# Sixteen output buffers in the weight staging tiles, and nine stores issued late

## Chip, core and metric

The kernel runs on one core of a Trainium2 chip. The metric is the device time of one execution in microseconds (us). TensorE (PE in the profile; its weight loads are PEld) multiplies matrices and writes PSUM, VectorE (DVE), ScalarE (ACT) and GpSimd (POOL) work on elements, and SyncE (SP) issues all DMAs, one after the other, each once the data that it moves is ready and the place that it writes is free.

## What is computed

A gated linear attention over 4 batches, 8 heads, 768 steps and a head width of 48, whose output is the input of a layer with a squared ReLU:

```python
for t in range(S):
    state = alpha[:, :, t, :, None] * state + np.einsum('bhd,bhe->bhde', k[:, :, t], v[:, :, t])
    y[:, :, t] = np.einsum('bhd,bhde->bhe', q[:, :, t], state)
...
x = np.ascontiguousarray(attn_out.transpose(0, 2, 1, 3)).reshape(B * S, H * D)
h = x @ w_in                # 3072 x 384 times 384 x 2048
r = np.maximum(h, 0.0)
g = s * (r * r) + b
return g @ w_out            # 3072 x 2048 times 2048 x 384
```

Inputs and output are float32; the kernel multiplies in bf16.

## The kernel before

The 3072 tokens are cut into 24 blocks of 128, six to a batch. The recurrence is done in blocks: cumulated products of alpha (`cumA`) scale q and k (`eb1`, `ei1`, then the multiplies `mul1` on line 609, which write the bf16 tile `qk`), the scores of a block are k times q under a triangular mask (`A1`, line 652, then `mk1`), and a state of 48 x 48 per head goes from block to block (`KV1`, `t1`, `sn`). The first eight blocks are handled in pairs by functions that end in 2 (`ld2`, `mul2`, `A2`, `mk2`, `y2`); from block 8 on each stands by itself. For the scores, q and k are needed with the head width on the partitions. For blocks 0 to 5 TensorE transposes them (`T2`); for blocks 6 and up a DMA transpose does, issued by SP (`T1`, line 630, from `qk` to `qkT`). `y1` forms the block's output in two PSUM banks and `ye` copies it to `xd`.

Blocks go through the layer two at a time (`GROUPS`). `mm1` multiplies by `w_in` into two PSUM banks `h_ps`, `re` (line 756) takes the ReLU into one of three tiles `r`, `sq` (line 775) squares it into `gt`. `mm2` (line 780) multiplies a block by `w_out` in four calls of four matmuls into `o_ps[n % 2]`. `oe(n)` (line 789, VectorE) scales that bank, adds the bias and writes it to an output buffer in SBUF, and `st(n)` stores the buffer: as two DMAs of 96 KB for blocks 0 to 7 (line 829), whose rows are interleaved, as one of 192 KB for the others (line 834). The last block is done in two halves of 192 columns (`mm2h`, `oeh`, `sth`). There are three output buffers `o_sb`, and block n uses the one with number n % 3, so `oe(n)` waits until `st(n - 3)` has landed.

The weights come in float32 through staging tiles: four tiles `wst` of 128 x 1536, of which the first two serve twice, and parts of two `gt` tiles. ScalarE, GpSimd and VectorE cast them to bf16 (`cih`, `co`) and sum `w_out` for the bias (`cp`). After about 44 us nothing touches `wst` any more.

The order of all this is written out by hand: the string `PROGRAM` lists every step, and a loop at the end of the kernel calls the function that each entry names (`mul1.q.12.DVE` is `mul1("q", 12, "DVE")`). Each engine runs its own instructions in that order and waits at each one for what it needs; the waits are derived from the regions of tiles that instructions read and write. Entries of different engines can change places in the string with no effect on either engine's order.

`F.n.w.bank` issues n matmuls of w columns on zeros into a bank that is rewritten afterwards: fillers, which keep TensorE at work while the first loads arrive.

Of the kernel before, what the change touches and what calls it, by code (L numbers as in the profile page):

```python
# [70 lines left out]
KV1.10 sq.3.3.0.ACT mm2.5.3 mul1.q.11.DVE re.3.2.1.1.ACT mm2.4.2 ld1.k.12 oe.5 sq.3.2.1.POOL mm2.4.3
ld1.v.11 t1.10 T1.11 A1.9 ln2.7 sn.10.POOL oe.4 mm2.7.0 mk1.9 mm2.7.1 ld2.a.11 mm2.6.0 ld1.k.13 st.3
mm2.6.1 Ayy.10 ld2.a.8 mm2.7.2 ld1.v.13 ye.8.DVE ye.9.ACT vc1.12.POOL mk1.10 mm1.4.1.0 vc1.11.POOL
mm1.4.2.1 re.4.1.0.2.ACT blk2.6 cumA.6 re.4.2.1.0.ACT A1.11 sq.4.2.0.DVE ei1.12 mm1.4.4.0 eb1.12
mul1.k.12.DVE mm1.4.3.1 eb1.13 mul1.q.12.DVE re.4.4.0.1.ACT mm2.6.2 mul1.q.13.DVE T1.12 el2.6
re.4.3.1.0.ACT sq.4.1.2.DVE mm1.4.0.0 sq.4.4.1.DVE sq.4.3.0.DVE mm1.4.6.1 re.4.0.0.2.ACT st.4 mk1.11
mm2.6.3 ei1.13 ld1.q.15 re.4.6.1.1.ACT mm1.4.7.0 sq.4.0.2.DVE ld1.v.14 oe.6 KV1.12 vc1.13.POOL mm2.7.3
t1.12 mm1.4.5.1 mul1.k.13.DVE mm2.8.0 T1.13 re.4.5.1.0.ACT Ayy.12 re.4.7.0.2.ACT oe.7 ld1.q.16 mm2.8.1
ld1.k.14 ye.10.DVE ye.11.ACT st.5 sq.4.5.0.DVE blk2.7 KV1.13 mk1.12 mm1.5.4.1 ld1.k.15 mm2.9.0 ld1.v.15
vc1.14.POOL re.5.4.1.0.ACT t1.13 mm1.5.5.0 sq.4.7.2.DVE mm1.5.6.1 sq.5.4.0.DVE re.5.5.0.2.ACT  # L80
sq.4.6.1.DVE cumA.7 sn.13.POOL ld1.v.16 A1.13 el2.7 mm1.5.3.0 re.5.6.1.0.ACT mk1.13 eb1.14 ld2.a.9
mm2.9.1 ei1.14 mul1.q.14.DVE ei1.15 mm2.8.2 re.5.3.0.1.ACT sq.5.6.0.DVE mm1.5.1.1 mul1.k.14.DVE eb1.15
sq.5.3.1.DVE mm2.8.3 T1.14 re.5.1.1.0.ACT mm1.5.0.0 sq.5.1.0.DVE sq.5.5.2.DVE mm1.5.2.1 st.7
re.5.0.0.1.ACT mul1.q.15.DVE mm2.9.2 oe.8 ld1.k.17 re.5.2.1.0.ACT sq.5.0.1.DVE st.6 KV1.14 mm1.5.7.0
mul1.k.15.DVE sq.5.2.0.DVE mm2.10.0 T1.15 re.5.7.0.2.ACT t1.14 mm2.10.1 sq.5.7.2.DVE sn.14.POOL mm2.10.2
ld1.k.16 ld2.a.10 Ayy.14 vc1.15.POOL ld1.v.22 ld1.q.17 mm2.10.3 ye.12.ACT mk1.14 vc1.16.POOL st.8
ye.13.ACT mm2.9.3 ln2.8 oe.10 KV1.15 mm1.6.4.1 t1.15 mm1.6.1.0 re.6.4.1.1.ACT sn.15.POOL blk2.8 cumA.8
re.6.1.0.0.ACT ld1.q.22 sq.6.4.1.DVE A1.15 eb1.16 mm1.6.3.1 oe.9 ei1.16 sq.6.1.0.DVE mm1.6.0.0
mul1.k.16.DVE re.6.3.1.2.ACT mul1.q.16.DVE mm2.11.0 el2.8 eb1.17 sq.6.3.2.DVE T1.16 re.6.0.0.1.ACT
mm2.11.1 mk1.15 ei1.17 mm1.6.2.1 sq.6.0.1.DVE ld1.v.17 mm2.11.2 re.6.2.1.0.ACT ld1.k.18 KV1.16 mm2.11.3  # L90
ld1.q.18 t1.16 st.10 mm1.6.6.0 oe.11 mm1.6.5.1 re.6.6.0.2.ACT mm2.13.0 ln2.10 sq.6.6.2.DVE mul1.q.17.DVE
mm1.6.7.0 re.6.5.1.1.ACT mul1.k.17.DVE Ayy.16 re.6.7.0.2.ACT T1.17 sq.6.7.2.DVE sq.6.2.0.DVE mm2.12.0
ye.14.ACT ye.15.DVE vc1.17.POOL ld1.v.18 ln2.9 mk1.16 sn.16.POOL mm2.13.1 ld1.q.23 ld1.q.19 mm1.7.0.1
sq.6.5.1.DVE ld1.k.19 blk2.9 mm1.7.4.0 re.7.0.1.2.ACT st.9 sq.7.0.2.DVE mm1.7.6.1 re.7.4.0.0.ACT
mm2.13.2 sq.7.4.0.DVE re.7.6.1.1.ACT cumA.9 A1.17 ld1.v.19 eb1.18 mm1.7.1.0 ei1.19 mul1.q.18.DVE
mm2.12.1 el2.9 eb1.19 mk1.17 vc1.18.POOL ei1.18 mm2.12.2 re.7.1.0.2.ACT mm1.7.7.1 mul1.k.18.DVE ln2.11
sq.7.1.2.DVE T1.18 mm2.13.3 re.7.7.1.0.ACT mm1.7.2.0 oe.13 mm2.12.3 ld1.k.20 mul1.q.19.DVE
re.7.2.0.2.ACT ld1.q.20 mm1.7.3.1 sq.7.2.2.DVE ld1.q.21 mul1.k.19.DVE mm2.15.0 re.7.3.1.2.ACT oe.12
vc1.19.POOL T1.19 mm1.7.5.0 sq.7.3.2.DVE KV1.18 mm2.14.0 re.7.5.0.2.ACT t1.18 st.11 mm2.14.1 ld1.k.21
sq.7.7.0.DVE sq.7.5.2.DVE Ayy.18 sq.7.6.1.DVE ld1.v.20 mm2.15.1 ye.16.ACT ye.17.DVE ld1.v.21 mk1.18  # L100
st.12 KV1.19 mm1.8.5.1 ld1.k.22 blk2.10 mm1.8.6.0 re.8.5.1.0.ACT t1.19 mm1.8.7.1 sq.8.5.0.DVE
re.8.6.0.2.ACT sn.19.POOL cumA.10 re.8.7.1.1.ACT A1.19 sq.8.6.2.DVE mm1.8.3.0 ei1.20 sq.8.7.1.DVE
mul1.k.20.DVE mm2.14.2 re.8.3.0.0.ACT mk1.19 mm1.8.2.1 el2.10 eb1.20 mm1.8.0.0 mul1.q.20.DVE
re.8.2.1.2.ACT vc1.20.POOL mm2.15.2 T1.20 eb1.21 re.8.0.0.1.ACT sq.8.2.2.DVE mm2.14.3 sq.8.3.0.DVE
ei1.21 sq.8.0.1.DVE mm1.8.1.1 ld1.k.23 mul1.k.21.DVE st.13 oe.14 vc1.21.POOL KV1.20 mm2.15.3
re.8.1.1.2.ACT mm1.8.4.0 sq.8.1.2.DVE oe.15 mm2.16.0 re.8.4.0.0.ACT mul1.q.21.DVE st.15 mm2.17.0 t1.20
T1.21 mm2.17.1 sq.8.4.0.DVE sn.20.POOL Ayy.20 ld1.v.23 st.14 mm2.17.2 ye.19.DVE vc1.22.POOL ye.18.DVE
mm2.17.3 mk1.20 KV1.21 blk2.11 mm1.9.5.1 t1.21 mm1.9.1.0 re.9.5.1.1.ACT sn.21.POOL A1.21 re.9.1.0.2.ACT
cumA.11 mm1.9.3.1 sq.9.5.1.DVE ei1.22 eb1.22 mul1.k.22.DVE mm2.16.1 re.9.3.1.0.ACT mul1.q.22.DVE
mm2.16.2 ei1.23 oe.17 T1.22 eb1.23 mm1.9.0.0 sq.9.3.0.DVE sq.9.1.2.DVE KV1.22 mul1.q.23.DVE mm2.16.3  # L110
re.9.0.0.1.ACT mm1.9.2.1 sq.9.0.1.DVE mk1.21 mm1.9.4.0 re.9.2.1.0.ACT mm2.19.0 mul1.k.23.DVE
re.9.4.0.2.ACT oe.16 mm1.9.7.1 el2.11 T1.23 sq.9.2.0.DVE mm1.9.6.0 t1.22 re.9.7.1.1.ACT mm2.18.0 st.16
sq.9.4.2.DVE re.9.6.0.0.ACT sn.22.POOL Ayy.22 vc1.23.POOL mm2.18.1 ye.21.DVE ye.20.DVE mm2.18.2
sq.9.7.1.DVE mm1.10.4.1 mk1.22 mm2.19.1 re.10.4.1.2.ACT sq.9.6.0.DVE mm1.10.1.0 A1.23 re.10.1.0.1.ACT
# [6 lines left out]
re.11.0.1.2.ACT mm2.21.3 sq.11.0.2.DVE re.11.3.0.1.ACT sq.11.7.0.DVE mm1.11.5.1 sq.11.3.1.DVE oe.21
mm1.11.4.0 re.11.5.1.2.ACT st.21 mm2.20.3 re.11.4.0.0.ACT mm2h.23.0.0 oe.20 mm2h.23.0.1 mm2h.23.1.1
sq.11.4.0.DVE st.20 mm2.22.0 sq.11.5.2.DVE mm2h.23.1.0 mm2.22.1 mm2.22.2 mm2.22.3 mm2h.23.2.0 oe.22
mm2h.23.3.0 mm2h.23.2.1 st.22 oeh.23.0 mm2h.23.3.1 sth.23.0 oeh.23.1 sth.23.1
# [4 lines left out]
def kernel(  # L129
# [657 lines left out]

    def oe(n):
        nc.vector.scalar_tensor_tensor(  # L789
            out=out_sb[n % 3],  # L790
            in0=o_ps[n % 2][:, 0:d_model],
            scalar=s_col,
            in1=bias_w,
            op0=ALU.mult,
            op1=ALU.add,
        )
# [13 lines left out]
    def oeh(n, h):  # L810
        w = slice(d_model // 2 * h, d_model // 2 * (h + 1))
        nc.vector.scalar_tensor_tensor(
            out=out_sb[n % 3][:, w],
            in0=(o_ps[1], ct_ps)[h][:, 0 : d_model // 2],
            scalar=s_col,
            in1=bias_w[:, w],
            op0=ALU.mult,
            op1=ALU.add,
        )
# [56 lines left out]
```

## Time and profile before

| | us |
|---|---|
| median of 3 runs | 185.15 (185.14 to 186.47) |
| the profiled execution | 184.67 |
| its span, first to last instruction | 183.0 |

The profile is of one execution. Its views used here are: the page (busy time of each engine, the span in 40 slices with the rate of DMA, and the chain of work that ended last); the busy time of each engine in chosen stretches, where a row has the stretch, its length, then for each engine the busy time and the number of instructions, the granted clock of TensorE as a share of full speed, the DMA share and GB/s; and the timeline, whose rows have the start, the duration, engine, line, operation, the tile written and the tiles read, the shapes, and how many such instructions follow each other. In square brackets stands how long the engine was idle before, and what released it; buffer numbers are left out. For SP a row is the issue of a DMA, not the transfer. A wait for several things is put down to the one that came last.

### The profile page before, as it was taken

How to read it: one execution, taken by the hardware profiler on the slowest of the kernel's cores; microseconds unless marked ns; L12 is line 12 of the kernel's file. 1: busy time of each engine (PE TensorE's matmuls, PEld its weight loads, DVE VectorE, ACT ScalarE, POOL GpSimd, SP SyncE). 2: the span in 40 equal slices, each digit the busy share in tenths (PEclk: the TensorE clock that was granted, in tenths of full speed). 3: DMA queues.
4: the chain of work that ended last, by engine and by line, in shares of the span. 5: the costliest groups of instructions: out<-in, count | busy, mean ns of one | idle time of the engine just before them, and what ended most of it. 6: DMA issues, size and time to landing. Idle time of an engine off the chain costs nothing.

```text
span 183.0 us, 5543 instructions
## 1 busy us (share of the span) xinstructions
PE 171.8 (94%) x2293; PEld 122.4 (67%) x2293; DVE 133.7 (73%) x257; ACT 103.8 (57%) x202; POOL 45.5 (25%) x81
## 2 busy tenths in 40 slices
PE   7868899999999999896999999999999999999993
PEld 2436686786567775684776677777776776687772
DVE  2599989999586786593987777677986896672423
ACT  3945888998727582662383757483571552263610
POOL 7447619340332534201303202110223103000000
PEclk9999999999999999999999999999999999999999
DMA  5999999999998989999989999888957323021022
GB/s 159 323 355 378 265 345 362 364 287 238 214 198 169 178 170 213 167 239 155 227 165 231 207 203 229 159 186 162 216 134 195 81 57 104 0 86 48 0 90 86
DMA packets 101357, 34.96 MB, mean 191 GB/s; under 512 B 94548, under 2 KB 99796, under 8 KB 101332
## 3 DMA queue, kind: packets, MB, share of 16 engines
q1 hardware_dynamic: 101332, 34.61, 79.5%
q8 instruction: 18, 0.29, 0.6%
q14 instruction: 7, 0.06, 0.1%
HBM read 25.17 MB, written 4.72 MB: 163 GB/s over the span
## 4 chain that ended last, share of the span: by engine, by line
PE 71%; SPq 11%; DMA 10%; DVE 4%; ACT 2%; issue 1%; ACTq 0%
PE o_ps L780 30%; PE h_ps L746 28%; SPq L299 9%; DMA qkT<-qk 6%; DMA wst<-in_moe_w_in_dram 4%; PE a_ps L652 2%; PE py_ps L674 2%; PE ct_ps L585 1%; PE ct_ps L674 1%; DVE colsum L364 1%; DVE qk L452 1%; SPq L325 1%; PE py_ps L639 1%; DVE gt L775 1%; ACT r L756 1%; SPq L312 1%
## 5 line engine op out<-in xcount | busy, mean ns | idle before, releaser
L756 ACT ACTIVATE r<-h_ps 128x512 bf16<-128x512 f32 x88 | 52.3, 599 | 49.0 <-PE h_ps L746 40.1
L746 PE MATMUL h_ps<-xd,w_in_bf 128*128 128x256 bf16 x576 | 74.2, 273 | 0.1
L780 PE MATMUL o_ps<-w_out_bf,gt 128*128 128x384 bf16 x368 | 69.9, 326 | 0.2 <-DVE gt L775 0.2
L746 PEld LDWEIGHTS <-w_in_bf 128*128 128x128 bf16 x576 | 54.1, 98 | 13.4 <-issue 1.3
L780 PEld LDWEIGHTS <-gt 128*128 128x128 bf16 x368 | 34.5, 98 | 18.9 <-DVE gt L775 0.5
L775 DVE TENSOR_TENSOR gt<-r 128x512 bf16<-128x512 bf16 x72 | 31.2, 452 | 12.1 <-ACT r L756 11.5
L725 POOL TENSOR_TENSOR s_st<-t,blast 128x384 bf16<-128x384 bf16 x15 | 13.5, 903 | 41.3 <-DVE t L715 33.2
L661 DVE TENSOR_TENSOR am<-a_ps,U 128x1024 bf16<-128x1024 f32 x16 | 19.5, 1218 | 2.7 <-PE a_ps L652 2.7
L789 DVE SCALAR_TENSOR_TENSOR o_sb<-o_ps,bs,bias_w 128x384 f32<-128x384 f32 x23 | 14.1, 615 | 8.0 <-PE o_ps L780 4.9
L340 POOL CAST vp<-v_in 128x384 bf16<-128x384 f32 x18 | 9.3, 522 | 35.8 <-DMA v_in<-in_v_dram 26.7
L399 ACT ACTIVATE la<-a_in 128x768 bf16<-128x768 f32 x12 | 10.1, 842 | 4.5 <-DMA a_in<-in_alpha_dram 4.5
L773 ACT ACTIVATE gt<-r 128x512 bf16<-128x512 bf16 x18 | 11.1, 625 | 0.3
L715 DVE TENSOR_TENSOR t<-py_ps,s_st 64x192 bf16<-64x192 f32 x26 | 9.1, 352 | 2.9 <-PE py_ps L639 2.5
L775 POOL TENSOR_TENSOR gt<-r 128x512 bf16<-128x512 bf16 x6 | 6.2, 1039 | 19.7 <-ACT r L756 19.7
L609 DVE TENSOR_TENSOR qk<-k_in,binv 128x384 bf16<-128x384 f32 x16 | 8.8, 553 | 1.9 <-ACT binv L599 1.8
L609 DVE TENSOR_TENSOR qk<-q_in,b_s 128x384 bf16<-128x384 f32 x16 | 8.7, 550 | 1.5 <-ACT b_s L595 1.5
L514 DVE TENSOR_TENSOR am<-a_ps,mask 128x1024 bf16<-128x1024 f32 x6 | 7.3, 1217 | 2.0 <-PE a_ps L501 1.9
L652 PE MATMUL a_ps<-qkT 64*128 64x128 bf16 x128 | 6.3, 218 | 2.4 <-DMA qkT<-qk 1.9
L652 PEld LDWEIGHTS <-qkT 64*128 64x128 bf16 x128 | 3.9, 94 | 6.6 <-DMA qkT<-qk 4.2
L452 DVE TENSOR_TENSOR qk<-q_in,b_s 128x384 bf16<-128x384 f32 x8 | 4.3, 551 | 4.2 <-ACT b_s L429 4.2
L340 DVE CAST xd<-ct_ps 128x384 bf16<-128x384 f32 x6 | 3.3, 555 | 5.2 <-PE ct_ps L674 5.2
L338 ACT ACTIVATE xd<-ct_ps 128x384 bf16<-128x384 f32 x6 | 2.9, 488 | 7.0 <-PE ct_ps L674 4.7
(123 smaller groups left out, 188.2 us busy)
## 6 DMA issues: line engine op xcount, KB each, us to landing
a_in<-in_alpha_dram SPq DMA_DIRECT2D x12, 384.0 KB, 4.6
wst<-in_moe_w_in_dram SPq DMA_DIRECT2D x4, 768.0 KB, 7.6
v_in<-in_v_dram SPq DMA_DIRECT2D x16, 192.0 KB, 4.0
k_in<-in_k_dram SPq DMA_DIRECT2D x16, 192.0 KB, 3.7
q_in<-in_q_dram SPq DMA_DIRECT2D x16, 192.0 KB, 3.9
out_dram<-o_sb SPq DMA_DIRECT2D x15, 192.0 KB, 2.3
out_dram<-o_sb SPq DMA_DIRECT2D x18, 96.0 KB, 3.0
q_in<-in_q_dram SPq DMA_DIRECT2D x4, 384.0 KB, 5.9
```

The lines of the kernel that those rows point to most:

```text
L299: nc.sync.dma_start(out=to[r], in_=of[r])
L340: {"DVE": nc.vector, "POOL": nc.gpsimd}[eng].tensor_copy(out=out, in_=in_)
L609: on(eng).tensor_tensor(out=half_of(qk, n)[:, "qk".index(x), :, 0:D], in0=half_of(ins[x], n).rearrange("a (h d) -> a h d", d=D), in1=half_ ...
L652: nc.tensor.matmul(out=a_ps[:, e, 128 * p : 128 * p + 128], lhsT=T[r, 1, p, :], rhs=T[r, 0, p, :], start=True, stop=True,)
L661: nc.vector.tensor_tensor(out=half_of(am, n).rearrange("a e p t -> a (e p) t"), in0=a_ps.rearrange("a e (p t) -> a (e p) t", t=128), in1=U ...
L725: on(eng).tensor_tensor(out=s_sb[n % 4], in0=t1_sb[n % 2], in1=bl.unsqueeze(2).to_broadcast([128, NP, 96]), op=ALU.mult,)
L746: nc.tensor.matmul(out=h_ps[w][:, i * n : (i + 1) * n], lhsT=w_in_bf[:, kk, 128 * j : 128 * (j + 1)], rhs=xd_sb[g % 3][:, kk, 0:n], start= ...
L756: nc.scalar.activation(out=r_sb[i], in_=h_ps[w], func=AF.Relu)
L773: nc.scalar.activation(out=unit_out(g, u), in_=r, func=AF.Square)
L775: on(eng).tensor_tensor(out=unit_out(g, u), in0=r, in1=r, op=ALU.mult)
L780: nc.tensor.matmul(out=o_ps[n % 2][:, 0:d_model], lhsT=gt_of(n)[:, j, c0 : c0 + C], rhs=w_out_bf[:, j, :], start=(j == 0), stop=(j == NJ - 1),
L789: nc.vector.scalar_tensor_tensor(out=out_sb[n % 3], in0=o_ps[n % 2][:, 0:d_model], scalar=s_col, in1=bias_w, op0=ALU.mult, op1=ALU.add,)
```

## The change

The three tiles `o_sb` are gone. Block n's output goes to a quarter of a staging tile, so there are sixteen places, and block n uses the place of block n - 16:

```diff
-    out_sb = many("o_sb", 3, [128, d_model], FP32)
...
+    def out_of(n):
+        return wst[n // 4 % NST][:, d_model * (n % 4) : d_model * (n % 4 + 1)]
+
     def oe(n):
         nc.vector.scalar_tensor_tensor(
-            out=out_sb[n % 3],
+            out=out_of(n),
...
-                    in_=out_sb[n % 3][64 * s : 64 * s + 64],
+                    in_=out_of(n)[64 * s : 64 * s + 64],
...
-            nc.sync.dma_start(out=dst, in_=out_sb[n % 3])
+            nc.sync.dma_start(out=dst, in_=out_of(n))
```

`oeh` and `sth` change in the same way. In `PROGRAM` the stores of blocks 0 to 8 (seventeen DMAs) move on SP's queue. The entries of SP, in their order, from the first store on, before and after (entries of the other engines left out; between block 16's transpose and block 13's store nothing of SP's order changes):

```diff
-ld1.q.13 st.0 ld1.q.9 ld1.v.12 ld1.q.10 ld1.k.11 ld1.k.10 T1.8 st.2 ld1.q.14 st.1 T1.9 ld2.a.7 ld1.q.12
-T1.10 ld1.k.12 ld1.v.11 T1.11 ld2.a.11 ld1.k.13 st.3 ld2.a.8 ld1.v.13 T1.12 st.4 ld1.q.15 ld1.v.14 T1.13
-ld1.q.16 ld1.k.14 st.5 ld1.k.15 ld1.v.15 ld1.v.16 ld2.a.9 T1.14 st.7 ld1.k.17 st.6 T1.15 ld1.k.16 ld2.a.10
-ld1.v.22 ld1.q.17 st.8 ld1.q.22 T1.16
+ld1.q.13 ld1.q.9 ld1.v.12 ld1.q.10 ld1.k.11 ld1.k.10 T1.8 ld1.q.14 T1.9 ld2.a.7 ld1.q.12
+T1.10 ld1.k.12 ld1.v.11 T1.11 ld2.a.11 ld1.k.13 ld2.a.8 ld1.v.13 T1.12 ld1.q.15 ld1.v.14 T1.13
+ld1.q.16 ld1.k.14 ld1.k.15 ld1.v.15 ld1.v.16 ld2.a.9 T1.14 ld1.k.17 T1.15 ld1.k.16 ld2.a.10
+ld1.v.22 ld1.q.17 ld1.q.22 T1.16
...
-st.13 st.15 T1.21 ld1.v.23 st.14 T1.22 T1.23 st.16 st.19 st.18
-st.17 st.21 st.20 st.22 sth.23.0 sth.23.1
+st.13 st.15 T1.21 st.0 ld1.v.23 st.2 st.14 st.1 T1.22 st.3 T1.23 st.4 st.16 st.5 st.19 st.7 st.18
+st.6 st.17 st.8 st.21 st.20 st.22 sth.23.0 sth.23.1
```

On TensorE two fillers change their number and width, the one ahead of `A2.0.1.o` and the one ahead of `T2.1.1.o1`; on VectorE, ScalarE and GpSimd every instruction keeps its place:

```diff
-F.2.504.a0 A2.0.1.o
+F.4.416.a0 A2.0.1.o
...
-F.2.504.c T2.1.1.o1
+F.4.384.c T2.1.1.o1
```

More of the change, by code (lines that the diff above doesn't have):

```diff
@@ L71 @@
[L71 to L114, printed above, removed]
@@ L121 @@
[L121 to L124, printed above, removed]
+ld1.q.14 mm1.3.1.0 t1.8 T1.9 mm1.3.6.1 oe.3 sn.8.POOL mm2.4.1 re.3.6.1.2.ACT ld2.a.7 KV1.9 sq.3.7.0.ACT
+blk2.5 sq.3.6.2.POOL ld1.q.12 mm1.3.0.1 t1.9 re.3.1.0.0.DVE mm2.5.0 sn.9.POOL re.3.0.1.2.ACT cumA.5
@@ new lines @@
+sn.13.POOL ld1.v.16 A1.13 el2.7 mm1.5.3.0 re.5.6.1.0.ACT mk1.13 eb1.14 ld2.a.9 mm2.9.1 ei1.14
+mul1.q.14.DVE ei1.15 mm2.8.2 re.5.3.0.1.ACT sq.5.6.0.DVE mm1.5.1.1 mul1.k.14.DVE eb1.15 sq.5.3.1.DVE
+mm2.8.3 T1.14 re.5.1.1.0.ACT mm1.5.0.0 sq.5.1.0.DVE sq.5.5.2.DVE mm1.5.2.1 ld1.k.17 re.5.0.0.1.ACT
+mul1.q.15.DVE mm2.9.2 oe.8 re.5.2.1.0.ACT sq.5.0.1.DVE KV1.14 mm1.5.7.0 mul1.k.15.DVE sq.5.2.0.DVE
+mm2.10.0 T1.15 re.5.7.0.2.ACT t1.14 mm2.10.1 sq.5.7.2.DVE sn.14.POOL mm2.10.2 ld1.k.16 ld2.a.10 Ayy.14
@@ new lines @@
+re.8.5.1.0.ACT t1.19 mm1.8.7.1 sq.8.5.0.DVE re.8.6.0.2.ACT sn.19.POOL cumA.10 re.8.7.1.1.ACT A1.19
+sq.8.6.2.DVE mm1.8.3.0 ei1.20 sq.8.7.1.DVE mul1.k.20.DVE mm2.14.2 re.8.3.0.0.ACT mk1.19 mm1.8.2.1 el2.10
+eb1.20 mm1.8.0.0 mul1.q.20.DVE re.8.2.1.2.ACT vc1.20.POOL mm2.15.2 T1.20 eb1.21 re.8.0.0.1.ACT
+sq.8.2.2.DVE mm2.14.3 sq.8.3.0.DVE ei1.21 sq.8.0.1.DVE mm1.8.1.1 ld1.k.23 mul1.k.21.DVE st.13 oe.14
+vc1.21.POOL KV1.20 mm2.15.3 re.8.1.1.2.ACT mm1.8.4.0 sq.8.1.2.DVE oe.15 mm2.16.0 re.8.4.0.0.ACT
@@ L125 @@
+st.21 mm2.20.3 re.11.4.0.0.ACT mm2h.23.0.0 oe.20 mm2h.23.0.1 mm2h.23.1.1 sq.11.4.0.DVE st.20 mm2.22.0
+sq.11.5.2.DVE mm2h.23.1.0 mm2.22.1 mm2.22.2 mm2.22.3 mm2h.23.2.0 oe.22 mm2h.23.3.0 mm2h.23.2.1 st.22
+oeh.23.0 mm2h.23.3.1 sth.23.0 oeh.23.1 sth.23.1
 """
```

67 lines of the change are left out of this document (50 added, 17 removed).

## The prediction

> **What bounds the kernel now.** I read the page first (busy shares, chain), then busy time by stage, then the timeline at each place where TensorE stood still, then the DMA queue there.
>
> ```profile
> span 183.0 us, 5543 instructions
> PE 171.8 (94%) x2293; PEld 122.4 (67%) x2293; DVE 133.7 (73%) x257; ACT 103.8 (57%) x202; POOL 45.5 (25%) x81
> GB/s 159 323 355 378 265 345 362 364 287 238 214 198 169 178 170 213 167 239 155 227 165 231 207 203 229 159 186 162 216 134 195 81 57 104 0 86 48 0 90 86
> PE 71%; SPq 11%; DMA 10%; DVE 4%; ACT 2%; issue 1%; ACTq 0%
> ```
>
> TensorE is busy for 94% of the span, and it carries 71% of the chain. What a change off TensorE can win is its idle time, so the stages come next (stretch, its length, then each engine's busy time):
>
> ```profile
> 30.74:46.46 15.72, 15.54 (x218) 11.60 (x219) 14.93 (x26) 14.21 (x28) 4.54 (x4) 1.00 1.07 297
> 46.46:76.70 30.24, 30.14 (x402) 20.13 (x401) 20.17 (x35) 16.09 (x33) 10.39 (x15) 1.00 0.97 186
> 76.70:180.00 103.30, 100.69 (x1228) 74.22 (x1228) 74.09 (x148) 51.49 (x102) 13.09 (x20) 1.00 0.66 142
> ```
>
> Idle TensorE: 15.72 - 15.54 = 0.18 us, 30.24 - 30.14 = 0.10 us, and 103.30 - 100.69 = 2.61 us. The granted clock is 1.00 throughout. So from 30.74 us on nothing off TensorE can give more than about 2.9 us. The timeline shows where the 2.61 us lie:
>
> ```profile
> 77.14 0.23 PEld L652 LDWEIGHTS <-qkT 64*128 64x128 bf16 x8 [0.92 <-DMA qkT<-qk]
> 77.14 0.40 PE L652 MATMUL a_ps<-qkT 64*128 64x128 bf16 x8 [0.53 <-DVE gt L775]
> 85.86 0.40 PE L652 MATMUL a_ps<-qkT 64*128 64x128 bf16 x8 [1.52 <-DMA qkT<-qk]
> 104.54 0.40 PE L652 MATMUL a_ps<-qkT 64*128 64x128 bf16 x8 [0.33 <-DMA qkT<-qk]
> ```
>
> All three are line 652, the scores of blocks 11, 12 and 15, and what they lack is the DMA transpose that makes qkT (line 630). At 77.14 the matmul row names a DVE square, which comes later in the program than these matmuls and cannot be what they need; the weight load's row names the transpose. Together: 0.53 + 1.52 + 0.33 = 2.38 us.
>
> **The stores leave the early queue.** SP issues its DMAs in program order, and these transposes stand behind stores (L829, a pair for each of blocks 0 to 7):
>
> ```profile
> 68.15 2.58 SPq L630 DMA_TRANSPOSE qkT<-qk  x1
> 72.08 1.89 SPq L630 DMA_TRANSPOSE qkT<-qk  x1
> ...
> 76.29 2.08 SPq L829 DMA_DIRECT2D out_dram<-o_sb  x2
> ...
> 79.98 2.49 SPq L630 DMA_TRANSPOSE qkT<-qk  x1
> ...
> 96.52 1.23 SPq L829 DMA_DIRECT2D out_dram<-o_sb  x2
> ...
> 98.43 1.31 SPq L829 DMA_DIRECT2D out_dram<-o_sb  x2
> 99.84 1.32 SPq L630 DMA_TRANSPOSE qkT<-qk  x1
> ```
>
> A transpose may go when DVE has written both halves of its qk (line 609). The last multiplies of blocks 10, 11, 12 and 15, in this order:
>
> ```profile
> 66.48 0.55 DVE L609 TENSOR_TENSOR qk<-q_in,b_s 128x384 bf16<-128x384 f32 x1
> 67.75 0.55 DVE L609 TENSOR_TENSOR qk<-q_in,b_s 128x384 bf16<-128x384 f32 x1
> 77.64 0.55 DVE L609 TENSOR_TENSOR qk<-q_in,b_s 128x384 bf16<-128x384 f32 x1
> 96.99 0.55 DVE L609 TENSOR_TENSOR qk<-k_in,binv 128x384 bf16<-128x384 f32 x1
> ```
>
> Block 10 is ready at 67.03 and was issued at 68.15; block 11 at 68.30 and 72.08; block 12 at 78.19 and 79.98; block 15 at 97.54 and 99.84. From issue to landing the transposes started between 70 and 90 us took
>
> ```profile
> DMA to landing us min/median/max: 5.0/5.4/5.8
> ```
>
> - Block 11: with stores 0, 1 and 2 gone, block 10's transpose goes at 67.03, and everything queued behind it, block 11's too, moves up by 68.15 - 67.03 = 1.12 us, to 70.96. Landed at the longest, 5.8: 76.8. TensorE would be there at 77.14 - 0.53 = 76.61. In before it took 5.1 (77.14 - 72.08), so 76.0. The 0.53 goes.
> - Block 12: store 3 (2.08 us) was in front. Ready 0.53 earlier with TensorE's own progress, 77.66; landed 5.8 later, 83.5; needed at 85.86 - 1.52 - 0.53 = 83.81. The 1.52 goes, with 0.3 to spare.
> - Block 15: stores 7 and 6 (1.23 + 1.31 us) were in front. Ready at 97.54 - 2.05 = 95.49, landed by 101.3 at the longest; needed at 104.54 - 0.33 - 2.05 = 102.16. The 0.33 goes.
>
> What is late next is block 13's transpose, whose scores then come 2.05 us earlier; it too stood behind a pair of stores, and I leave 0.1 us for it (from 0, if it lands like its neighbours, to the 0.53 of the smallest like row).
>
> The loads that stood behind the nine stores also go out earlier. Their order and buffers are as before; what they meet is less traffic, since 17 DMAs leave this stretch.
>
> **The sixteen buffers.** Evictions 3 to 15 lose their wait for a store. One such wait shows, for block 7's eviction:
>
> ```profile
> 86.44 0.62 DVE L789 SCALAR_TENSOR_TENSOR o_sb<-o_ps,bs,bias_w 128x384 f32<-128x384 f32 x1 [2.62 <-DMA out_dram<-o_sb]
> ```
>
> It lies under TensorE's wait that ended at 85.86, so by itself it counts nothing; had it stayed it would have been the next to be late.
>
> **The late stores.** Seventeen issues go behind block 21's transpose. Six matter, two each for blocks 0, 2 and 1, beside the load and the store that stood there. Evictions 16 and 17 write over blocks 0 and 1 and now wait for those stores.
>
> ```profile
> 138.71 1.24 SPq L630 DMA_TRANSPOSE qkT<-qk  x1
> 140.04 0.54 SPq L288 DMA_DIRECT2D v_in<-in_v_dram  x1
> 140.64 0.57 SPq L834 DMA_DIRECT2D out_dram<-o_sb  x1
> 146.40 5.09 SPq L630 DMA_TRANSPOSE qkT<-qk  x2
> ...
> 146.41 0.62 DVE L789 SCALAR_TENSOR_TENSOR o_sb<-o_ps,bs,bias_w 128x384 f32<-128x384 f32 x1
> ...
> 150.12 0.61 DVE L789 SCALAR_TENSOR_TENSOR o_sb<-o_ps,bs,bias_w 128x384 f32<-128x384 f32 x1
> ...
> 151.43 0.81 PE L780 MATMUL o_ps<-w_out_bf,gt 128*128 128x384 bf16 x4
> ...
> 152.18 0.40 PE L652 MATMUL a_ps<-qkT 64*128 64x128 bf16 x8
> ```
>
> The stores of two DMAs each (duration of the issue, then from issue to landing):
>
> ```profile
> L829 SPq DMA_DIRECT2D out_dram<-o_sb x16: 587/592/2002, 52.6 to 99.1; - x16
> ...
> DMA to landing us min/median/max: 2.2/3.2/3.7
> ```
>
> SP was idle from 141.21 to 146.40. From 139.95, at 0.59 us an issue and its gap (six of them, 3.6) with the load and store between (0.54 + 0.57), block 1's second store goes at about 144.2 and the stretch ends at 144.8, before block 22's transpose is due. It lands 2.2 to 3.7 later, 146.4 to 147.9; eviction 17 (146.41) so waits 0 to 1.5 us. Behind it on DVE are squares, block 23's multiplies and a mask, without a gap up to eviction 16 (ends 150.73), whose bank the matmuls at 151.43 need: slack 0.70. The cost on TensorE is 0 to 0.8 us; with the median landing of 3.2 it is 0.3. Traffic is thinner here (81 and 57 GB/s in the slices after 142 us, against 150 to 240 where those rows were taken), so I take 0.1.
>
> The Trainium skill (DMA: Bandwidth & Descriptors, Anatomy of one DMA) gives a DMA a fixed cost of about 2.0 us, most of it the receipt of the last write. By that block 1 would land at 146.2 and the wait would cost nothing, and the sum would be 0.1 us better; the rows above say 2.2 to 3.7.
>
> Block 3's pair goes between the last two transposes (5.09 us for two, so time for 1.2 us of issue); blocks 4 to 8 fill waits of SP for late evictions, and their buffers are written again only from eviction 20 on.
>
> **The fillers.** 4 x 416 and 4 x 384 columns replace 2 x 504 twice: 656 and 528 columns more. From
>
> ```profile
> 46.46 2.76 PE o_ps L780 x16
> ```
> ```profile
> 10.60 0.42 PE L501 MATMUL o_ps<-qkT 64*64 64x128 bf16 x16 [0.84 <-DVE qkT L340]
> ...
> 13.53 0.62 PE L464 MATMUL o_ps<-ident,qk 128*128 128x128 bf16 x8 [0.63 <-POOL qk L452]
> ```
>
> 2.76 us for 16 x 384 columns, they are 0.29 and 0.24 us. The matmuls behind them wait 0.84 and 0.63 us for DVE and GpSimd, so they cost nothing; uncovered it would be 0.53 us, in a stage that waits for loads anyway. The order of work on DVE, ACT and GpSimd does not change: where the list moves their entries it moves them past other engines' entries only.
>
> **The sum.** 2.38 - 0.1 - 0.1 = 2.18 us. The profiled execution took 184.67 us (span 183.0 and 1.67 around it) and would take 182.5. The median of the runs, 185.15, lies 0.48 above it; from there 182.97, so 183.0.
>
> **The rivals.** (1) Transposes paced by the loads. The same loads stay in front of them; if these, not the stores, set their landing, block 11's 0.53 stays, and the rest of 1.85 loses up to 0.8 to eviction 17: 1.05 us won, 184.1. For it: landings of 5.0 to 5.8 us against an issue of 2. Against it: block 12's transpose alone is held for 1.79 us after its data is ready.
>
> (2) Slower: the late stores choke SP. At 76.29 a pair took 2.08 us to issue, not 1.2. At that pace three pairs, the load and the store take 3 x 2.08 + 1.1 = 7.3 us, block 1's second store goes at about 146.2 and, landing after 3.7, frees eviction 17 at 149.9: 3.5 us late, of which 0.70 is slack; the last transposes slip 0.9 and a landing of 5.8 (147.3 + 5.8 = 153.1) then adds up to 0.9 at the scores of block 22 (152.18). Cost 2.8 to 3.7, or 185.6 to 186.5; the gain is gone from a pair of about 1.9 us on. At the pace of the slowest single issue of such a store (2.00) the six alone take 12 us, 8.3 more than forecast, and eviction 17 would be about 8.3 + 1.5 late: 9.8 - 0.7 - 2.28 = 6.8 us over, 192. Between these I set the case at 187.5. Against it: 0.54 and 0.57 us for the issues at 140 us, and the traffic there. The Trainium skill (same page, Queues, rings and completion order) says that descriptors of one issuing engine are consumed in ring order, which would put the transposes behind those stores' bytes; by the rows above that is within the slack unless the issues stretch.
>
> (3) The sharing of a tile makes false waits: if a write to one quarter of a staging tile waited for stores of another, the last eviction would wait for the store before it, some 2 to 4 us at the end, 185 to 187. The last rows speak against it:
>
> ```profile
> 179.66 1.00 SPq L823 DMA_DIRECT2D out_dram<-o_sb  x2
> 179.87 0.42 DVE L812 SCALAR_TENSOR_TENSOR o_sb<-ct_ps,bs,bias_w 128x192 f32<-128x192 f32 x1 [0.24 <-PE ct_ps L802]
> ```
>
> DVE writes one half of a buffer 0.21 us after the store of the other half began, so waits go by region.
>
> **How the numbers follow.** The forecast has 0.60, within 182.5 to 183.6; the first rival 0.29, the second 0.09, the third 0.02. A change of 1%, 1.85 us, is about what a measurement of this kernel can tell from none: the bounds are 183.30 and 187.00. Of the forecast 0.52 lies below 183.30. Faster 0.52; within 1% 0.08 of the forecast, the 0.29 and 0.01 of the second rival: 0.38; slower 0.10. The range goes from 182.3 (all 2.61 and a little noise) to 184.9, which takes in the first rival and leaves out the slower ones and a little at each end.
>
> **What would show it.** Right: no wait for qkT on TensorE between 75 and 105 us, 0.4 us of idle TensorE or less from 76.7 to 180, transposes issued as their multiplies end. Wrong: waits for qkT that stay; a wait of eviction 16 or 17 for a store with TensorE idle behind it near 150 us; late issues of over 1 us each; evictions near the end waiting for stores.

## The result, and the profile after

| | before | after |
|---|---|---|
| median, us | 185.14 (184.31 to 186.47, 6 runs) | 182.87 (182.28 to 183.43, 6 runs) |
| the profiled execution, us | 184.67 | 183.43 |
| its span, us | 183.0 | 181.7 |

The changed kernel takes 0.9856 of the time of the kernel before, with a 95% interval of 0.982 to 0.9891: faster by 1.4%, against 183.0 us and 1.2% forecast. A few executions of some kernels lie more than 1.5% above that kernel's fastest; the medians count them, the ratios and their intervals do not. Line numbers after the declaration of the output buffers differ by a line or more: the scores are line 651 now, the transposes 629, the evictions 792, the stores of two DMAs 832.

The page of the changed kernel: span, busy time of each engine, and the chain that ended last, by engine.

```profile
span 181.7 us, 5539 instructions
PE 171.4 (94%) x2297; PEld 123.0 (68%) x2297; DVE 134.0 (74%) x257; ACT 103.5 (57%) x202; POOL 46.5 (26%) x81
PE 82%; DVE 8%; DMA 3%; issue 3%; SPq 1%; ACT 1%; DVEq 0%; ACTq 0%
```

SP's queue and the DMAs, 21% of the chain before, are 4% of it now. The busy times are nearly the same, so what went is waiting. Where it went shows between two points that both programs pass: the start of the scores of block 10 and of block 23. First the kernel before, then the changed one, in the table of stretches (stretch, length, then busy time of PE, PEld, DVE, ACT, POOL, granted clock, DMA share, GB/s):

```profile
72.64:156.77 84.13, 81.59 (x1082) 59.57 (x1082) 64.77 (x125) 44.07 (x89) 14.10 (x21) 1.00 0.85 171
```

```profile
74.20:155.55 81.35, 81.33 (x1081) 59.71 (x1081) 65.27 (x125) 43.92 (x89) 14.60 (x21) 1.00 0.77 168
```

This stretch is 2.78 us shorter, and TensorE's idle time in it fell from 84.13 - 81.59 = 2.54 us to 0.02. The spans differ by 1.3 only, because this execution came to block 10 1.56 us later (74.20 against 72.64). That early part differs from run to run: in the other profiles of this study, whatever the kernel, block 10's scores began between 73.36 and 76.17, and once at 80.12. Much of it in this pair is one gap in a row of small matmuls that update the state: TensorE stands still for 1.75 us ahead of the one at 18.90, and for 0.23 us ahead of the same one in the kernel before (17.01). The profile names nothing that it waited for, and the other profiles have from 0.45 to 1.97 us there, so the cause stays open. The medians, of six runs each, average over it; so in the experiments I compare stretches that begin at block 10.

The timeline of TensorE in the changed kernel, at the three scores that waited before:

```profile
78.00 0.39 PE L651 MATMUL a_ps<-qkT 64*128 64x128 bf16 x8
85.13 0.40 PE L651 MATMUL a_ps<-qkT 64*128 64x128 bf16 x8
...
103.31 0.39 PE L651 MATMUL a_ps<-qkT 64*128 64x128 bf16 x8
```

No bracket stands behind any of them: the waits of 0.53, 1.52 and 0.33 us are gone. SP's timeline says why:

```profile
71.26 1.62 SPq L629 DMA_TRANSPOSE qkT<-qk  x1
...
74.18 2.80 SPq L298 DMA_DIRECT2D a_in<-in_alpha_dram  x1
77.02 1.07 SPq L287 DMA_DIRECT2D v_in<-in_v_dram  x1
79.81 1.25 SPq L629 DMA_TRANSPOSE qkT<-qk  x1
...
96.87 1.24 SPq L629 DMA_TRANSPOSE qkT<-qk  x1
```

Block 12's transpose is the one at 79.81. SP is done with the load ahead of it at 78.09 and stands idle until the multiply has written qk; then the transpose goes within 0.1 us. Before, the same transpose was issued 1.79 us after its data was ready and took 2.49 us to issue. SP no longer runs behind its data here. Block 11's transpose still does: its data was ready at 69.86, it went at 71.26, behind two loads, and landed after 3.5 us, in time for the scores at 78.00. Over all transposes whose landing the profile has, landings came sooner (minimum, median, maximum; before it was 2.7, 4.2, 5.8):

```profile
DMA to landing us min/median/max: 2.7/2.9/4.5
```

**What the change costs.** DVE's timeline around eviction 17, which writes over block 1's output:

```profile
144.25 0.55 DVE L608 TENSOR_TENSOR qk<-q_in,b_s 128x384 bf16<-128x384 f32 x1
145.95 0.62 DVE L792 SCALAR_TENSOR_TENSOR wst<-o_ps,bs,bias_w 128x384 f32<-128x384 f32 x1 [1.14 <-DMA out_dram<-wst]
...
147.62 0.42 DVE L774 TENSOR_TENSOR gt<-r 128x512 bf16<-128x512 bf16 x1
...
149.55 0.61 DVE L792 SCALAR_TENSOR_TENSOR wst<-o_ps,bs,bias_w 128x384 f32<-128x384 f32 x1
```

The eviction waits 1.14 us for block 1's store. On SP that pair was issued late and slowly:

```profile
138.44 1.21 SPq L832 DMA_DIRECT2D out_dram<-wst  x2
139.76 0.53 SPq L287 DMA_DIRECT2D v_in<-in_v_dram  x1
140.34 1.35 SPq L832 DMA_DIRECT2D out_dram<-wst  x2
141.73 0.59 SPq L837 DMA_DIRECT2D out_dram<-wst  x1
142.36 1.90 SPq L832 DMA_DIRECT2D out_dram<-wst  x2
```

TensorE feels it twice, by amounts too small to leave a bracket, since a matmul's modelled end runs into the next start:

```profile
148.09 0.82 PE L779 MATMUL o_ps<-w_out_bf,gt 128*128 128x384 bf16 x4
148.75 1.47 PE L745 MATMUL h_ps<-xd,w_in_bf 128*128 128x256 bf16 x12
150.22 0.81 PE L779 MATMUL o_ps<-w_out_bf,gt 128*128 128x384 bf16 x4
```

The matmuls at 148.09 start right after the square that ends at 147.62 + 0.42 = 148.04, and those at 150.22 right after eviction 16 has freed their bank, at 149.55 + 0.61 = 150.16. Counted from the scores of block 21, the matmuls at 148.09 come 0.19 us later than their like before (5.59 against 5.40), and those at 150.22 0.36 (7.72 against 7.36). From the scores of block 21 to those of block 22 it takes 150.96 - 142.50 = 8.46 us, against 8.11 before: 0.35 lost.

The differences between successive scores (before minus after) add up like this: 0.70 to block 11, 1.59 to block 12, 0.49 to block 15, 0.32 to block 17, -0.35 to block 22, and 0.03 in small ones: 2.78.

### The profile page after: what moved, and what is told of

Same layout as the page of the kernel before. It is cut to its first block, busy times and chain, and to the rows that moved or that the text cites. A ratio compares the mean times of both kernels' runs of the same rounds, so it can differ in the third digit from the quotient of the medians.

```text
span 181.7 us, 5539 instructions
## 1 busy us (share of the span) xinstructions
PE 171.4 (94%) x2297; PEld 123.0 (68%) x2297; DVE 134.0 (74%) x257; ACT 103.5 (57%) x202; POOL 46.5 (26%) x81
## 4 chain that ended last, share of the span: by engine, by line
PE 82%; DVE 8%; DMA 3%; issue 3%; SPq 1%; ACT 1%; DVEq 0%; ACTq 0%
PE o_ps L779 33%; PE h_ps L745 32%; DMA k_in<-in_k_dram 3%; PE a_ps L651 3%; PE py_ps L673 2%; DVE qk L451 2%; PE ct_ps L584 2%; PE ct_ps L673 2%; DVE am L513 1%; DVE colsum L363 1%; PE py_ps L638 1%; SPq L298 1%; DVE qkT L339 1%; PE ct_ps L419 1%; PE a_ps L500 1%
## 5 line engine op out<-in xcount | busy, mean ns | idle before, releaser
L792 DVE SCALAR_TENSOR_TENSOR wst<-o_ps,bs,bias_w 128x384 f32<-128x384 f32 x23 | 14.2, 615 | 6.4 <-PE o_ps L779 4.9
L608 DVE TENSOR_TENSOR qk<-k_in,binv 128x384 bf16<-128x384 f32 x16 | 9.4, 590 | 1.9 <-ACT binv L598 1.8
L339 DVE CAST xd<-py_ps 128x384 bf16<-128x384 f32 x8 | 4.4, 553 | 3.0 <-PE py_ps L673 2.9
L841 PE MATMUL a_ps<-zeros 128*128 128x504 bf16 (+3 forms) x18 | 5.4, 443 | 1.3 <-DVE zeros L217 1.3
```

The source lines that it names most:

```text
L339: {"DVE": nc.vector, "POOL": nc.gpsimd}[eng].tensor_copy(out=out, in_=in_)
L608: on(eng).tensor_tensor(out=half_of(qk, n)[:, "qk".index(x), :, 0:D], in0=half_of(ins[x], n).rearrange("a (h d) -> a h d", d=D), in1=half_ ...
L792: nc.vector.scalar_tensor_tensor(out=out_of(n), in0=o_ps[n % 2][:, 0:d_model], scalar=s_col, in1=bias_w, op0=ALU.mult, op1=ALU.add,)
```

## The experiments

Edits of the order are shown as SP's entries alone. "10 to 21" is the time from the scores of block 10 to those of block 21, in the profiled execution, and "21 to 23" the rest of the way to block 23's; ratios are to the runs of the kernel before that were taken beside each kernel, whose medians were 185.93 to 186.03 in the experiments and 185.14 for the changed kernel.

| kernel | 10 to 21 | 21 to 23 | median, us | ratio, 95% interval |
|---|---|---|---|---|
| before | 71.43 | 12.70 | 185.14 | 1 |
| after | 68.30 | 13.05 | 182.87 | 0.9856 (0.982, 0.9891) |
| new fillers only | 71.64 | 12.70 | 186.15 | 1.0021 (0.9981, 1.0061) |
| old fillers | 68.31 | 12.98 | 182.99 | 0.9867 (0.9817, 0.9917) |
| buffers only | 71.98 | 12.70 | 186.69 | 1.0057 (1.0013, 1.0101) |
| order only | 80.40 | 12.71 | 195.64 | 1.0557 (1.0463, 1.0651) |
| store 3 back | 68.31 | 12.89 | 185.95 | 0.9891 (0.98, 0.9981) |
| store 3 back, repeated | 68.30 | 12.85 | 182.63 | 0.9839 (0.9788, 0.989) |
| stores 0 to 2 back | 68.31 | 12.70 | 183.01 | 0.9881 (0.9811, 0.9951) |
| stores 0 to 3 back | 69.34 | 12.70 | 184.57 | 0.9956 (0.9918, 0.9995) |
| buffers only, small stores | 71.19 | 12.70 | 185.36 | 0.9954 (0.9909, 0.9998) |
| no early stores | 68.30 | 12.70 | 182.51 | 0.9844 (0.9786, 0.9902) |
| stores 0 to 2 sooner | 68.39 | 12.70 | 182.57 | 0.9852 (0.9803, 0.9901) |
| stores 0 to 2 later | 68.31 | 20.41 | 190.36 | 1.0274 (1.0197, 1.0351) |

### The fillers

The kernel before with the new fillers:

```diff
-F.2.504.a0 A2.0.1.o
+F.4.416.a0 A2.0.1.o
...
-F.2.504.c T2.1.1.o1
+F.4.384.c T2.1.1.o1
```

> The kernel before with the two fillers of the changed kernel and nothing else. My theory (the gain is the stores leaving the early queue): no change, 185.1 us within 0.5, ratio 0.997 to 1.003, the three waits for qkT still there. Rival (fillers): the changed kernel reaches block 10's scores 1.56 us later than the kernel before (74.20 against 72.64 in their profiles); if the fillers do that, this kernel takes 186 to 187 us, ratio about 1.008.

And the changed kernel with the old ones:

```diff
-F.4.416.a0 A2.0.1.o
+F.2.504.a0 A2.0.1.o
...
-F.4.384.c T2.1.1.o1
+F.2.504.c T2.1.1.o1
```

> The changed kernel with the two fillers of the kernel before. My theory: as the changed kernel, ratio to the kernel before 0.983 to 0.988. Rival (fillers): they cost up to 1.5 us in the changed kernel, and without them the ratio is 0.976 to 0.980 (181.0 to 181.6 us).

Neither moves the time by what can be measured. With the new fillers alone block 12 still waits (TensorE's timeline):

```profile
87.38 0.40 PE L652 MATMUL a_ps<-qkT 64*128 64x128 bf16 x8 [1.49 <-DMA qkT<-qk]
```

The waits move about among the others from run to run (0.34 at block 11, 0.23 at block 14, 0.79 at block 15 here). Their sum is 2.85 us against 2.38, and the way from block 10 to 21 takes 71.64 against 71.43. The fillers are no part of the gain.

### The buffers alone, and the order alone

The changed kernel with the order and the fillers of before, so that the stores go early again (SP's entries; the order of the other engines is that of before too):

```diff
-T1.8 ld1.q.14 T1.9 ld2.a.7 ld1.q.12
+T1.8 st.2 ld1.q.14 st.1 T1.9 ld2.a.7 ld1.q.12
...
-T1.21 st.0 ld1.v.23 st.2 st.14 st.1 T1.22 st.3 T1.23 st.4 st.16 st.5
+T1.21 ld1.v.23 st.14 T1.22 T1.23 st.16
```

> The sixteen places in the staging tiles, with stores and fillers in the order of before. My theory: the wait of block 7's eviction (2.62 us on DVE) goes, the waits of TensorE for the transposes of blocks 11, 12 and 15 stay at about 0.5, 1.5 and 0.3 us, time as before within 0.4 us. Rival (the gain comes from evictions that need not wait for a store): most of the gain is here, 183.0 to 183.5 us.

TensorE's timeline there, at the scores of blocks 11 and 12:

```profile
79.65 0.40 PE L651 MATMUL a_ps<-qkT 64*128 64x128 bf16 x8 [0.48 <-DMA qkT<-qk]
88.30 0.40 PE L651 MATMUL a_ps<-qkT 64*128 64x128 bf16 x8 [1.44 <-DMA qkT<-qk]
```

The eviction's wait for a store is gone, the waits for transposes are all there (block 15's, 1.12 us, is larger than before), and the time is not better; the interval even says slower by 0.1 to 1.0%. About 0.4 us of that lies outside the span: 188.11 - 186.0 = 2.1 us in the profiled execution and 2.0 to 2.2 in all the runs, as in the kernel with small stores below, where the other kernels have 1.6 to 1.9. I cannot explain it.

The other half: the three buffers of before, and seven of the nine stores behind the transpose that they held up. It is a milder order than that of the changed kernel, which three buffers cannot hold: block 3's eviction would wait for block 0's store, and that would stand behind the transposes of much later blocks.

```diff
-st.0 ld1.q.9 ld1.v.12 ld1.q.10 ld1.k.11 ld1.k.10 T1.8 st.2 ld1.q.14 st.1 T1.9
+ld1.q.9 ld1.v.12 ld1.q.10 ld1.k.11 ld1.k.10 T1.8 st.0 ld1.q.14 T1.9 st.2 st.1
...
-ld1.k.13 st.3 ld2.a.8 ld1.v.13 T1.12 st.4 ld1.q.15 ld1.v.14 T1.13
+ld1.k.13 ld2.a.8 ld1.v.13 T1.12 st.3 ld1.q.15 ld1.v.14 T1.13 st.4
...
-T1.14 st.7 ld1.k.17 st.6 T1.15
+T1.14 ld1.k.17 T1.15 st.6 st.7
```

> The kernel before, three buffers, with the stores of blocks 0 to 4, 6 and 7 moved just behind the transpose that stood behind them. It tests whether the order alone does it. Theory (the queue as a whole is behind, and a store moved by one place still stands ahead of all the later transposes; with three buffers evictions wait for the stores): waits for qkT stay or come back as waits of evictions for stores; 184.5 to 187 us. Rival (what counts is the store directly ahead of a transpose): the three waits go, 183.0 to 183.5 us.

It is 5.6% slower. The transposes meet no scores that wait for them, but DVE waits for buffers and TensorE for DVE. Evictions on DVE's timeline, then TensorE's:

```profile
88.38 0.62 DVE L789 SCALAR_TENSOR_TENSOR o_sb<-o_ps,bs,bias_w 128x384 f32<-128x384 f32 x1 [3.72 <-DMA out_dram<-o_sb]
94.65 0.62 DVE L789 SCALAR_TENSOR_TENSOR o_sb<-o_ps,bs,bias_w 128x384 f32<-128x384 f32 x1 [4.42 <-DMA out_dram<-o_sb]
```

```profile
89.05 1.44 PE L780 MATMUL o_ps<-w_out_bf,gt 128*128 128x384 bf16 x4 [2.37 <-DVE o_sb L789]
...
95.79 0.48 PE L639 MATMUL py_ps<-vp,qk 128*128 128x96 bf16 x4 [2.24 <-DVE xd L340]
```

The direction was expected, the size was not: behind the stalls of 2.37, 2.24 and 1.83 us the clock drops too (last section). Against the changed kernel 3.17 us are lost up to block 12's scores, 4.96 up to block 13's, and 2.01 and 1.82 up to those of blocks 15 and 16. So neither half wins alone: the order needs the places, and the places by themselves save a wait that cost nothing.

### Which stores held the transposes up

The prediction put block 12's wait down to store 3, which stands two loads ahead of its transpose. The changed kernel with store 3 back in its old place:

```diff
-ld1.k.13 ld2.a.8
+ld1.k.13 st.3 ld2.a.8
...
-T1.22 st.3 T1.23
+T1.22 T1.23
```

> The changed kernel with block 3's store back in its old place, ahead of the loads and the transpose of block 12; all else as changed. My theory: block 12's transpose goes out 1 to 2 us after its multiplies end and TensorE waits 0.5 to 1.5 us for it, so 0.5 to 1.5 us slower than the changed kernel. Rival (the loads ahead of it set its landing, or the total of bytes): no wait comes back with one store of nine, time as the changed kernel within 0.3 us.

No wait shows. But in the profiled execution TensorE came to block 10's scores only at 80.12, 4 to 7 us later than in the other kernels, so that SP may have been ahead for that reason alone. The same kernel was run once more.

> The same kernel as e4 once more, since in the profiled execution of e4 TensorE reached block 10's scores 6 us later than in the others and the queue was ahead for that reason alone. My theory as before: TensorE waits 0.5 to 1.5 us for block 12's transpose, and from the scores of block 10 to those of block 23 it takes 81.9 to 82.9 us (81.35 in the changed kernel, 84.13 before). Rival, which e4 speaks for: no wait, 81.3 to 81.5 us, since one store of nine is too little to bring the queue behind.

It costs nothing: the median is 182.63, and block 12's scores do not wait. SP's timeline there:

```profile
74.13 2.48 SPq L832 DMA_DIRECT2D out_dram<-wst  x2
76.65 0.59 SPq L298 DMA_DIRECT2D a_in<-in_alpha_dram  x1
77.28 0.70 SPq L287 DMA_DIRECT2D v_in<-in_v_dram  x1
79.14 1.27 SPq L629 DMA_TRANSPOSE qkT<-qk  x1
```

The pair takes 2.48 us, much as before (2.08), but SP is through at 77.98, ahead of the multiply (79.06), and still idles for 1.16 us. Without the pair the load of alpha at 74.18 took 2.80 us in the same place. So what SP issues at that time is slow, store or load; the store itself adds little here.

Stores 0, 1 and 2 back instead:

```diff
-ld1.q.13 ld1.q.9
+ld1.q.13 st.0 ld1.q.9
...
-T1.8 ld1.q.14 T1.9
+T1.8 st.2 ld1.q.14 st.1 T1.9
...
-T1.21 st.0 ld1.v.23 st.2 st.14 st.1 T1.22
+T1.21 ld1.v.23 st.14 T1.22
```

> The changed kernel with the stores of blocks 0, 1 and 2 back in their old places, all else as changed. My theory: block 11's transpose goes out about 1.1 us later than need be and TensorE waits 0.3 to 0.7 us for it; eviction 17 no longer waits for block 1's store, which gives back 0.35 us near 150 us; from block 10's scores to block 23's about 81.5 us. Rival (the backlog of the queue adds up over all stores): waits come back at blocks 12 and 15 too, 82.5 us or more.

No wait shows here either, though block 11's transpose was issued at 71.97 and landed 5.5 us later, at 77.47, when TensorE came to it at 77.56. All four:

```diff
-ld1.q.13 ld1.q.9
+ld1.q.13 st.0 ld1.q.9
...
-T1.8 ld1.q.14 T1.9
+T1.8 st.2 ld1.q.14 st.1 T1.9
...
-ld1.k.13 ld2.a.8
+ld1.k.13 st.3 ld2.a.8
...
-T1.21 st.0 ld1.v.23 st.2 st.14 st.1 T1.22 st.3 T1.23
+T1.21 ld1.v.23 st.14 T1.22 T1.23
```

> The changed kernel with the stores of blocks 0 to 3 back in their old places. Block 3's store alone (e4b) and those of blocks 0 to 2 alone (e5) brought no wait back. Theory (the backlog of the queue adds up): four pairs together bring it back, block 12's transpose goes out 0.7 us or more after its multiplies end and TensorE waits 0.5 to 1.7 us for it; from block 10's scores to block 23's 81.5 to 82.8 us. Rival (the pairs of blocks 4 to 7 are what does it): no wait, about 81.0 us.

Now a wait is back. By the ratio most of the gain is lost (0.9956, where the changed kernel has 0.9856); the profiled execution is one of the faster (183.95 us) and loses less, 82.04 us from block 10 to block 23 against 81.35 and 84.13. The runs that the ratio counts go from 183.69 to 185.35 us, so how much is lost is not settled. TensorE's and SP's timelines:

```profile
78.72 0.40 PE L651 MATMUL a_ps<-qkT 64*128 64x128 bf16 x8 [0.86 <-DMA qkT<-qk]
```

```profile
73.14 2.15 SPq L629 DMA_TRANSPOSE qkT<-qk  x1
...
79.97 0.60 SPq L287 DMA_DIRECT2D v_in<-in_v_dram  x1
80.69 2.42 SPq L629 DMA_TRANSPOSE qkT<-qk  x1
```

The wait is block 11's, and its transpose (73.14, landing after 5.5 us) goes before store 3 does; block 12's goes 1.25 us after its data (79.44), but lands in 4.4 and makes no one wait.

How many pairs it takes is not shown by this. Up to block 11's transpose SP's order is the same with stores 0 to 2 back and with all four. Yet the transpose went 1.78 us ahead of block 10's scores in the one execution (71.97 against 73.75) and 0.75 in the other (73.14 against 73.89). That microsecond is a matter of the run. What the profiles do show is this:

- After block 10 no scores wait for a transpose in the kernels with no pair early, with one (store 3) and with three (stores 0 to 2). With four pairs one wait shows. All four kernels with the full early order have three or four: before, with the new fillers, with the buffers only, and with small stores (below).
- Block 15's wait is in these four alone (0.33, 0.79, 1.12 and 1.20 us). With stores 0 to 3 early and 4 to 8 late it is gone.
- Block 12's wait of about 1.5 us did not come back with four pairs, although SP's order up to its transpose is that of the kernel before. What differs is behind it: in the kernel before, store 4 is issued next, while the transpose is still under way. From issue to landing, first before, then with the four stores back:

```profile
DMA to landing us min/median/max: 5.8/5.8/5.8
```
```profile
DMA to landing us min/median/max: 4.4/4.4/4.4
```

With the new fillers it is 5.6 and with the buffers only 5.5, both with store 4 behind it; with small stores, where store 4 has an eighth of its bytes, 4.4. So what is issued behind a transpose seems to lengthen its landing by over 1 us. No run tests store 4 by itself.

The delay thus belongs to SP's queue and the traffic as a whole, and comes out at whichever transpose has the least time.

Is it the bytes? The kernel with the buffers only, whose stores of blocks 0 to 7 write 48 of the 384 columns: as many DMAs and rows, an eighth of the bytes.

```diff
-                    out=dst.rearrange("(p s) m -> s p m", s=2)[s],
-                    in_=out_of(n)[64 * s : 64 * s + 64],
+                    out=dst.rearrange("(p s) m -> s p m", s=2)[s][:, 0:48],
+                    in_=out_of(n)[64 * s : 64 * s + 64, 0:48],
```

> The sixteen buffers with the order of before (as e3), but the stores of blocks 0 to 7 write only 48 of their 384 columns, so that the rest of these rows of the output is not written: as many DMAs and as many rows, an eighth of the bytes. Theory A (the time of SP and of the descriptors to issue each store is what holds the queue): waits as in e3, 84 to 84.7 us from block 10's scores to block 23's. Theory B (the bytes on the DMA engines are): the backlog goes, no wait for qkT, 81.0 to 81.5 us.

SP's timeline at store 3 and block 12's transpose:

```profile
77.27 1.79 SPq L832 DMA_DIRECT2D out_dram<-wst  x2
...
80.67 2.46 SPq L629 DMA_TRANSPOSE qkT<-qk  x1
```

Issues are as slow as with full stores, and from block 10 to block 21 it takes 71.19 us: 0.79 better than with full stores (71.98), 2.89 worse than with no early stores (68.30). The waits now are 0.78 us at block 11, 0.49 at block 14 and 1.20 at block 15; block 12's is gone. By this stretch the bytes are about a fifth of what the stores cost, and part of the 0.79 may be the run, since the three kernels with full early stores lie between 71.43 and 71.98. The ratios make the share of the bytes larger: 1.0057 with full stores, 0.9954 with small ones, 0.9844 with none, which is about half. So a good part of the cost, from half to four fifths, goes with the DMAs and rows; the split is not settled, and which of the two, DMAs or rows, was not tried.

### Where the late stores should go

The changed kernel with the stores of blocks 0 to 8 left out:

```diff
-T1.21 st.0 ld1.v.23 st.2 st.14 st.1 T1.22 st.3 T1.23 st.4 st.16 st.5 st.19 st.7 st.18
-st.6 st.17 st.8 st.21
+T1.21 ld1.v.23 st.14 T1.22 T1.23 st.16 st.19 st.18
+st.17 st.21
```

> The changed kernel with the stores of blocks 0 to 8 left out, so that these rows of the output are not written. It prices the late stores. My theory: eviction 17 does not wait (1.14 us on DVE in the changed kernel) and 0.35 us of TensorE's time between the scores of blocks 21 and 22 goes (8.46 us in the changed kernel, 8.11 in the kernel before); 81.0 us from block 10 to block 23, and 0.3 to 0.5 us less in all. Rival (late stores cost more by sharing the DMA engines, or nothing): 1 us or more, or no difference.

From block 10 to 21 it equals the changed kernel (68.30), and from 21 to 23 it has the 12.70 of before: so the late stores cost 0.35 us of TensorE's time, all at eviction 17.

Stores 0 to 2 earlier:

```diff
-ld1.k.22 T1.20 ld1.k.23 st.13 st.15 T1.21 st.0 ld1.v.23 st.2 st.14 st.1 T1.22
+ld1.k.22 st.0 st.2 T1.20 ld1.k.23 st.13 st.15 T1.21 st.1 ld1.v.23 st.14 T1.22
```

> The changed kernel with the stores of blocks 0 and 2 ahead of block 20's transpose and that of block 1 right behind block 21's, about 2 to 7 us sooner; all else as changed. My theory: they fill idle time of the queue there, eviction 17 finds its place free, and the stretch from block 21's scores to block 22's goes from 8.46 back to 8.11 us; 0.35 us faster than the changed kernel. Rival: the pairs now hold up block 20's transpose and a wait for qkT appears there, time as the changed kernel or slower.

Eviction 17 no longer waits (12.70), 0.09 us is lost on the way, and the stretch is 81.09 against 81.35. The median, 182.57, and its interval cannot be told from those of the changed kernel. And later, behind block 22's transpose:

```diff
-T1.21 st.0 ld1.v.23 st.2 st.14 st.1 T1.22 st.3 T1.23
+T1.21 ld1.v.23 st.14 T1.22 st.0 st.2 st.1 st.3 T1.23
```

> The changed kernel with the stores of blocks 0, 2 and 1 behind block 22's transpose, in that order, instead of ahead of it. It tests the slack that I gave eviction 17. From 146.1 us three pairs of 1.2 us end at 149.8; block 1 lands 2.2 to 3.2 us after its second store, near 151.5 us, so eviction 17 starts 6 to 7 us later than without a wait, and block 23's transpose slips as well. Theory (slack 0.70 us, then TensorE waits one for one): the stretch from block 21's scores to block 22's goes from 8.46 to 13 to 14.5 us and the kernel takes 187 to 189 us. Rival (the evictions have far more slack, as 0.35 us lost for 1.14 us of waiting may be taken): under 2 us lost.

Slower than before by 2.7%. DVE's and TensorE's timelines, and TensorE's stretches:

```profile
150.77 0.62 DVE L792 SCALAR_TENSOR_TENSOR wst<-o_ps,bs,bias_w 128x384 f32<-128x384 f32 x1 [6.79 <-DMA out_dram<-wst]
```

```profile
152.91 1.46 PE L779 MATMUL o_ps<-w_out_bf,gt 128*128 128x384 bf16 x4 [5.67 <-DVE gt L774]
```

```profile
147.24:152.91 5.67, 0.00 (x0) 0.01 (x1) 2.14 (x6) 1.10 (x3) 0.00 (x0) 0.74 0.49 120
152.91:156.41 3.50, 3.50 (x15) 2.22 (x16) 3.44 (x7) 0.65 (x2) 0.28 (x1) 0.50 0.23 52
```

Eviction 17 waits 6.79 us. What TensorE then lacks is not the bank but a square (`gt`) queued on DVE behind the eviction, and the matmuls after it run at half the clock. From block 21 to block 22 it takes 157.48 - 141.67 = 15.81 us, 7.70 more than without a wait: 5.67 idle and about half of the 4 us or so after it. I had reckoned with the wait alone, which was too little.

## Why the prediction came out

- **The gain is the waits for transposes: right.** They were 0.53 + 1.52 + 0.33 = 2.38 us and gave 0.70 + 1.59 + 0.49 = 2.78; each gap gave a little more than its bracket. Two of the signs named for it are there in full: no wait for qkT, and 0.02 us of idle TensorE from block 10 to block 23. The third is there for blocks 10, 12, 13 and 15, whose transposes were issued as their multiplies ended, but not for block 11, which was 1.40 us late and had the time.
- **The stores hold the transposes, not the loads (first rival): right in the main.** With the same loads in front, the waits are there with nine early stores and gone with none. But loads are issued slowly too (2.80 us for alpha at 74.18), and no run took loads away, so what they add is not shown.
- **The step that failed: "Block 12: store 3 (2.08 us) was in front".** I took the delay of a transpose to be the issue time of the stores just ahead of it, for all three blocks, and kept the landing of 5.0 to 5.8 us, which rested on two transposes. Store 3 put back alone costs nothing, and four pairs put back bring 0.86 us at block 11, ahead of store 3, and none at block 12. In place of that step stands a backlog of the whole queue with the traffic around it. In the kernel before, block 11's and 12's transposes took 1.89 and 2.49 us to issue and 5.0 and 5.8 to land; in the changed one 1.62 and 1.25 to issue, 3.5 and 2.7 to land. For block 15 the step holds: its wait is there with pairs 4 to 7 early and gone without them. Since all nine stores left, the sum came out all the same, and that is luck in part: the three gaps gave 0.40 us more than I counted and block 13 took 0.1 less, and eviction 17 cost 0.25 more.
- **Block 13's 0.1 us** did not come: its transpose was issued at once, and no wait is left.
- **Eviction 17, put at 0.1 us, measured 0.35.** The mechanism and the slack of 0.70 were right in the main (1.14 - 0.70 = 0.44 against 0.35), though 0.19 of the 0.35 came at a square that I had not priced. What was mis-sized is the issue: the three pairs took 1.21, 1.35 and 1.90 us where I had 1.2, and block 1's store, landing after 2.9, kept the eviction waiting 1.14 us: inside the 0 to 1.5 given for that wait, above what 0.1 allowed for. The Trainium skill (DMA: Bandwidth & Descriptors, Anatomy of one DMA), by whose 2.0 us there was to be no wait, gives that figure for DMAs issued from GpSimd, while SP issues these. It fits the median of the late stores, 2.2 us, better than this pair.
- **The 0.32 us at block 17** were not foreseen. They fall where two squares took longer in the profile of before (1.41 us, 1.01 after). The kernel with the new fillers alone, which has the stores early, does not have them (5.78 us there, as after). So they seem to belong to that one execution rather than to the change, and the part of the 2.78 that the change owns is nearer 2.5.
- **Fillers and buffers: at nothing, right.** The waits by region too: no eviction waited for another quarter's store near the end, so the third rival is dead. The second rival, late stores that choke SP, did not come: three pairs took 4.46 us to issue, not 3 x 2.08. One of its signs, a late issue of over 1 us, did show (1.51 us at the longest). A cost of its size was one move away, by another way: with the stores one transpose later (190.36) SP issues eight DMAs in 5.05 us, at its usual pace, and eviction 17 waits for them all the same.
